# A fused attention and gated MLP kernel on one core: output tiles of 16 by 8 tokens stored by one transfer each, more places for the first chunk's output, and the last accumulator finished by halves

## The chip, the core and the metric

The kernel runs on one core of one Trainium2 chip. The metric is the device time of one execution in microseconds (us). Five engines run side by side, each with its own instruction queue that is worked off in order: TensorE (PE, matmuls; its weight loads are listed as PEld), VectorE (DVE), ScalarE (ACT), GpSimd (POOL) and SyncE (SP). SP computes nothing: it issues nearly all DMA transfers of this kernel. A few transfers are issued from ACT's queue.

## What is computed

Two steps in float32. First an attention over 8 batches, 8 heads, 576 positions and 64 columns per head, that adds a coarse part and a local part. Then its output, seen as 4608 tokens of 512 values, goes through a gated MLP with 2048 hidden units.

```python
# attention, per head: q, k, v are (576, 64)
q_d, k_d, v_d = (t.reshape(144, 4, 64).mean(1) for t in (q, k, v))
out_up    = repeat(softmax(q_d @ k_d.T / 8) @ v_d, 4)          # coarse part
out_local = softmax(where(|i - j| < 4, q @ k.T / 8, -1e9)) @ v  # band of 7
x = (out_up + out_local)          # -> (8 * 576 tokens, 8 * 64 = 512)
# MLP
h = x @ w_in                      # (4608, 2048)
g = h * clip(h + 3, 0, 6) / 6
out = g @ w_out                   # (4608, 512)
```

## The kernel before

**Chunks.** The MLP works on nine chunks of 512 tokens. Chunks 0 to 6 go through `plan_moe` one after the other; the tokens that are left, two chunks' worth, go together through `plan_strassen`, a block multiplication with seven products, which ends the program. The attention of a batch (576 tokens) must be done before the chunk that needs it, and its matmuls come in short bursts between the MLP's matmuls.

**Tokens and batches.** The attention writes a batch transposed: `xt[b]` has the columns of a pair of heads on the partitions and the 576 tokens along the row, in 16 runs (`NC`) of 36 tokens (`RP`). Two places hold batches (`xb`, the first 9216 bytes of each partition and the 9216 behind it): batch 0's leftovers and then the even batches lie in the first one, named `first` in the trace, and the odd batches in the second, named `arena` there as nearly everything else is. Chunk n takes tokens 512 n to 512 n + 511 in order, so that its tokens come from one or two batches.

**Splitting a chunk.** All big matmuls are made of three with rounded operands: x is split into a rounded part and the rest (`plan_split`; the matmuls stay exact enough by hi·hi + hi·lo + lo·hi). For each half of the 512 columns (`k` in steps of two blocks of 128) and each batch in the chunk there is one copy (hi, on ACT or DVE, line 120 or 122) and one subtraction (lo, line 976, on DVE or POOL) into the tile `rounded`. The split waits for the last first-layer matmul of the chunk before, half by half.

**A chunk.** For 16 blocks `f` of 128 hidden units: 12 matmuls into one of two accumulators `h0`, `h1` (line 1060), ACT and DVE make g from it and split it (lines 1066 to 1078), and two blocks later 12 matmuls add its share to the four output accumulators `o0` to `o3` (line 1119), one for each tile of 128 tokens. The attention bursts use `h0` and `h1` too, and free them with the additions of line 757 on DVE.

**Storing.** `plan_store` copies an output accumulator to a place `ob` (lines 1022 on ACT, 1024 on DVE), of which there are two, and SP stores it from there. In DRAM the tokens lie as 36 by 32 rows: token r of run c is row 32 r + c. So a tile of 128 consecutive tokens is stored in pieces that end where a run of 36 ends, four or five transfers a tile (line 1036). A place is free, and the next accumulator can be copied, when its transfers have landed; an accumulator is free for the next chunk when it has been copied.

**The order.** `Plan.emit` plays the program through with costs and due times and writes every engine's queue in the order that it finds. DVE, ACT, POOL and SP work strictly in that order. Operations whose cost table names two engines (`on(...)`) go to the one that is free first. So an edit moves instructions in places that it does not touch. Other work in these queues: `plan_sum` adds weight blocks for the later block multiplication (lines 1177 and 1182) in a place of its own, `so`, and stores them (line 1189, to `si` and `so` in DRAM); the next sum can start when that store has landed. q and k are loaded at line 323 and turned on DVE at line 329.

**The end.** In the block multiplication the second layer ends in accumulators of 128 output columns by 512 tokens. The last product (`plan_units(4, ..., 2)`) adds eight blocks of three matmuls (line 1624) to two accumulators, named `o` in the trace; then `finish` turns each on DVE in two halves of 256 tokens (line 1576), and `plan_out` stores it in four transfers of 32 columns by 512 tokens (line 1589), two from SP and two from ACT, each of which waits for both halves.

Of the kernel before, what the change touches and what calls it, by code (L numbers as in the profile page):

```python
# [8 lines left out]
F32 = mybir.dt.float32  # L9
# [47 lines left out]
def tile_local_down_attention_moe(ctx, tc, q_all, k_all, v_all, _qk_loc, _v_loc, w_in, w_out, ident_d, _mask_d, out):  # L57
# [882 lines left out]
    def x_of(n, b, k, ks, s0, cnt):  # L940
        if n == PAIR0 - 1 and b == B - 2:
            return runs(b, k, ks)[:, :, :EDGE, :LONG]
        if b:
            return xt[b][:, k:k + ks, s0:s0 + cnt]
        return x0[k][:, s0:s0 + cnt].unsqueeze(1) if n == 0 else xt[0, "tail"][:, k:k + ks]

# [4 lines left out]
    def pieces(n):  # L951

        first, size = PART[n]
        if n == 0:
            return [(0, 0, 0, HALF), (0, HALF, HALF, TOK - HALF)]
        out_, t = [], first
        while t < first + size:
            b, s0 = divmod(t, S)
            k = min(S - s0, first + size - t)
            out_.append((b, s0, t - first, k))  # L960
            t += k
        return out_

    def plan_split(n, prev_last):

        ks = 1 if n == 0 else 2

        def part(i, b, k, off, cnt):
            x = parts_of(n)[i][:, k:k + ks, off:off + cnt]
            return x.rearrange("p k (c r) -> p k c r", r=LONG) if n == PAIR0 - 1 and b == B - 2 else x  # L970

        def hi(eng, b, s0, off, cnt, k):
            copy_on(eng, part(0, b, k, off, cnt), x_of(n, b, k, ks, s0, cnt))

        def lo(eng, b, s0, off, cnt, k):
            eng.tensor_tensor(
                part(1, b, k, off, cnt), x_of(n, b, k, ks, s0, cnt), part(0, b, k, off, cnt).bitcast(F32),
                op=ALU.subtract)

        done = []  # L980
        for k in range(0, NK, ks):
            for b, s0, off, cnt in pieces(n):
                free = [("x0", (0, k))] if n == 0 else []
                a = op(on("xhi", ks * cnt), 0, lambda eng, a=(b, s0, off, cnt, k): hi(eng, *a),
                       [x for h in range(k, k + ks) for x in x_done[b, h][s0 // HALF if n == 0 else 0:][:1 if n == 0 else None]]
# [5 lines left out]
                if n and s0 + cnt == S:  # L991
                    last_split.setdefault(b, []).append(c)
        split_done[n] = done
        for b, s0, _, cnt in pieces(n):
            if n and s0 + cnt == S:
                plan.free_after(xb_of(b), last_split[b])
# [1207 lines left out]
```

## Time and profile before

| | |
|---|---|
| median of three runs | 895.48 us |
| the three runs | 895.33, 895.48, 899.03 us |
| the profiled execution | 898.18 us |
| its span, first to last instruction | 896.3 us |
| mean granted TensorE clock in it | 0.996 |
| PE busy | 876.3 us (98%) |
| DVE, ACT, POOL busy | 658.4, 491.2, 291.5 us |
| DMA queue of SP | 354680 packets, 134.48 MB |

The span is what the profiler's views cover; the 1.9 us up to the execution's own time lie around it. A row of a view by lines gives the line in the source, the engine, the operation, the tile written and the tiles read, how many there were, their busy time and the mean of one. A row of the timeline gives the start and the length in us; the bracket at its end is idle time of that engine just before, and what ended it. "SPq" and "ACTq" are transfers being issued by those queues, not the transfers themselves. In a table by stretches each engine has its busy microseconds with the number of instructions behind it, then the granted clock, the share of the 16 DMA engines and what they moved.

### The profile page before, as it was taken

To read this page: it belongs to the slowest core of one execution; us is meant where nothing else is said; L and a number is where in the kernel's file an instruction comes from. 1 tells how busy PE (TensorE), PEld (TensorE's weight loads), DVE (VectorE), ACT (ScalarE), POOL (GpSimd) and SP (SyncE) were. 2 spreads that over 40 slices of the span, in tenths; PEclk is the share of its full clock that TensorE was granted. 3 is DMA by queue.
4 is the path that set the end of the run, shared out by engine and by line. 5 is a ranking of instruction groups with operands and counts; after the bars stand their busy time and mean duration, and the time that the engine had idled before them with its cause. 6 is when DMAs were issued, how large, how long until landed. Compare 5 with 4: busy or idle time off the path is not lost.

```text
span 896.3 us, 19849 instructions
## 1 busy us (share of the span) xinstructions
PE 876.3 (98%) x6913; PEld 714.8 (80%) x6913; DVE 658.4 (73%) x1224; ACT 491.2 (55%) x1542; POOL 291.5 (33%) x383
## 2 busy tenths in 40 slices
PE   6999999999999999999999999999999999999997
PEld 5667778788888888878888888888888888888786
DVE  7898876566666777667857776676757777778983
ACT  4799866455664545535455555454443426556760
POOL 3645542135443342234403351333312111013321
PEclk9899999999999999999999999999999999999999
DMA  9999753456566664656565654777855117564784
GB/s 221 289 221 250 178 141 66 99 116 119 114 142 131 139 143 114 134 124 136 120 139 122 147 124 100 135 213 217 209 130 136 36 37 232 206 218 145 267 266 62
DMA packets 361052, 137.59 MB, mean 154 GB/s; under 512 B 270456, under 2 KB 333048, under 8 KB 360952
## 3 DMA queue, kind: packets, MB, share of 16 engines
q1 hardware_dynamic: 354680, 134.48, 61.1%
q10 hardware_dynamic: 6272, 1.84, 0.9%
q8 instruction: 55, 0.90, 0.4%
q14 instruction: 45, 0.37, 0.1%
HBM read 91.62 MB, written 44.63 MB: 152 GB/s over the span
## 4 chain that ended last, share of the span: by engine, by line
PE 88%; DVE 5%; DMA 2%; SPq 1%; ACT 1%; issue 1%; ACTq 0%; DVEq 0%
PE o L1119 32%; PE h L1060 31%; PE h L1374 4%; PE a L1374 4%; PE o L1624 4%; PE o L1475 2%; PE a L709 2%; PE h L752 1%; PE a L1624 1%; PE h L1624 1%; PE a L501 1%; PE h L664 1%; DMA arena<-in_k_dram 1%; SPq L323 1%; DMA out_dram<-arena 1%
## 5 line engine op out<-in xcount | busy, mean ns | idle before, releaser
L1119 PE MATMUL o<-wp,rounded 128*128 128x512 f32 x1344 | 324.1, 393 | 2.6 <-DVE arena L1024 1.5
L1060 PE MATMUL h<-rounded,wp 128*128 128x512 f32 x1344 | 316.8, 390 | 2.4 <-DVE first L757 1.7
L1060 PEld LDWEIGHTS h<-rounded,wp 128*128 128x128 f32 x1344 | 251.2, 188 | 56.5 <-issue 3.2
L1119 PEld LDWEIGHTS o<-wp,rounded 128*128 128x128 f32 x1344 | 249.5, 188 | 56.7 <-DVE arena L1024 1.9
L1074 ACT CAST rounded<-arena 128x512 fp32r<-128x512 f32 x112 | 69.1, 617 | 73.1 <-PE o L1119 39.9
L1066 ACT ACTIVATE arena<-h 128x512 f32<-128x512 f32 x112 | 66.5, 594 | 75.2 <-PE h L1060 72.4
L1070 DVE SCALAR_TENSOR_TENSOR arena<-arena,h 128x512 f32<-128x512 f32 x112 | 75.8, 678 | 43.2 <-ACT arena L1066 42.5
L1078 DVE TENSOR_TENSOR rounded<-arena,rounded 128x512 fp32r<-128x512 f32 x83 | 60.9, 735 | 42.5 <-PE o L1119 33.2
L565 ACT ACTIVATE arena<-arena 128x64 f32<-128x64 f32 x240 | 80.3, 337 | 0.4
L1078 POOL TENSOR_TENSOR rounded<-arena,rounded 128x512 fp32r<-128x512 f32 x29 | 38.8, 1338 | 70.3 <-PE o L1119 45.2
L329 DVE STREAM_TRANSPOSE arena<-arena 128x576 f32<-128x576 f32 x56 | 43.3, 773 | 20.2 <-DMA arena<-in_q_dram 9.7
L1182 POOL TENSOR_TENSOR arena<-arena 128x128 f32<-128x128 f32 x57 | 31.5, 553 | 76.6 <-DVE arena L1182 33.7
L378 POOL TENSOR_TENSOR arena<-arena 128x144 f32<-128x144 f32 x30 | 13.5, 451 | 111.7 <-DVE arena L329 78.7
L422 POOL TENSOR_TENSOR arena<-arena 32x256 f32<-32x256 f32 (+1 forms) x27 | 22.9, 847 | 72.1 <-DMA arena<-in_v_dram 52.0
L541 ACT ACTIVATE arena<-arena 128x1 f32<-128x1 f32 (+1 forms) x78 | 15.1, 193 | 56.2 <-DVE arena L554 56.2
L565 ACT ACTIVATION_READ_ACCUMULATOR arena<-arena 128x1 f32 x240 | 45.2, 188 | 0.0
L684 ACT ACTIVATE arena<-h 128x144 f32<-128x144 f32 x24 | 7.0, 290 | 66.0 <-PE h L664 66.0
L582 DVE TENSOR_TENSOR arena<-arena 128x640 f32<-128x640 f32 (+1 forms) x43 | 37.5, 875 | 1.1
L380 POOL TENSOR_TENSOR arena<-arena 128x144 f32<-128x144 f32 x60 | 35.4, 590 | 4.7
L1374 PE MATMUL a<-wp,wp 128*128 128x512 f32 x144 | 36.5, 390 | 0.4 <-DVE arena L1404 0.4
L420 DVE TENSOR_REDUCE arena<-arena 128x128 f32<-128x512 f32 (+1 forms) x25 | 26.6, 1066 | 8.0 <-PE h L664 4.1
L1374 PEld LDWEIGHTS a<-wp,wp 128*128 128x128 f32 x144 | 27.0, 188 | 6.3 <-DVE arena L1404 0.8
(281 smaller groups left out, 1385.4 us busy)
## 6 DMA issues: line engine op xcount, KB each, us to landing
rawp<-in_w_in_dram SPq DMA_DIRECT2D x16, 512.0 KB
rawp<-in_w_out_dram SPq DMA_DIRECT2D x16, 512.0 KB
arena<-in_q_dram SPq DMA_DIRECT2D x112, 72.0 KB
arena<-in_k_dram SPq DMA_DIRECT2D x112, 72.0 KB
pl<-arena SPq DMA_DIRECT2D x24, 320.0 KB
arena<-pl SPq DMA_DIRECT2D x96, 80.0 KB
arena<-in_v_dram SPq DMA_DIRECT2D x28, 256.0 KB
wd<-wp SPq DMA_DIRECT2D x12, 512.0 KB
```

The source lines that it names most:

```text
L329: nc.vector.transpose(out=qk[kind], in_=qk[kind])
L380: eng.tensor_tensor(t, t, x[:, :, r], op=ALU.add)
L565: nc.scalar.activation(x[:, j], x[:, j], AF.Exp, bias=m[:, j:j + 1], scale=0.125, accum_out=s[:, j:j + 1])
L582: eng.tensor_tensor(x, x, s.unsqueeze(2).broadcast_to(list(x.shape)), op=ALU.mult)
L1060: nc.tensor.matmul(st["ps"], win[f][:, wt, kk * P:(kk + 1) * P], xs[part][:, kk], start=(kk == 0 and i == 0), stop=(kk == NK - 1 and i == ...
L1066: nc.scalar.activation(st["t"], st["ps"], AF.Relu, bias=3.0)
L1070: nc.vector.scalar_tensor_tensor(out=t, in0=t, scalar=6.0, in1=st["ps"], op0=ALU.min, op1=ALU.mult)
L1074: nc.scalar.copy(st["gh"], st["t"])
L1078: eng.tensor_tensor(st["gl"], st["t"], st["gh"].bitcast(F32), op=ALU.subtract)
L1119: nc.tensor.matmul(otile[n, m], gt[:, ms], wout[f][:, wt], start=(f == 0 and i == 0), stop=(f == NF - 1 and i == 2),)
L1374: nc.tensor.matmul(ps, weight(i, j, wt, kk), xpart(MOVING[j], part)[:, kk], start=first and kk == 0 and x == 0, stop=kk == half - 1 and x ...
L1624: nc.tensor.matmul(places[acc, m], w, z[:, part], start=j == 5 and i == 0 and x == 0, stop=i == NG - 1 and x == 2, skip_group_check=True)
```

## The change

**Blocks.** From batch 1 on a batch is cut along its runs instead of along its tokens: four blocks of 16 runs by 8 tokens (128 tokens), and a rest of 16 runs by 4 tokens (64 tokens). `_regions()` deals them out to chunks 1 to 6; the rests of two neighbouring batches lie side by side and fill a tile of 128. Batch 0 keeps its layout (chunk 0, and its last 64 tokens in chunk 1), and so does what chunk 6 takes of batch 6. Every chunk takes as many tokens from each batch as it did. An output tile of one block goes out in one transfer of 16 by 8 rows, and a pair of rests in two.

**Splits.** `split_ops(n)` makes one copy and one subtraction for each single block or rest (both column blocks of a half at once), and one for each column block where two or three blocks of a batch lie side by side. For chunks 1 to 6 these are 8, 6, 10, 8, 10 and 6 pairs of operations, where there were 4 each.

**Places.** The first chunk's output gets a list of places of its own, `ob0`: the two of `ob` and four more in the place of the even batches.

**The end.** The last product finishes its first accumulator, then adds the last five blocks to the second accumulator in two passes, one for each half of 256 tokens. Each half is turned when its pass is done and is stored in four transfers of 32 columns by 256 tokens.

```diff
+    def regions(n):
+        got = []
+        for off, b, j in REGIONS[n]:
+            if j in range(NC) and got and got[-1][0] == b and got[-1][1] in range(NC):
+                got[-1][2] += 1
+            else:
+                got.append([b, j, 1, off])
+        return got
...
+    def split_ops(n):
...
+                x = runs(b, k, ks)[:, :, :, j * BLOCK:(j + nj) * BLOCK]
+                return x if nj == 1 else x[:, 0].rearrange("p c (j r) -> p j c r", r=BLOCK)
...
+        return [cols(b, j, nj, off, k, ks) for kh in range(0, NK, 2) for b, j, nj, off in regions(n)
+                for ks in [1 if nj > 1 else 2] for k in range(kh, kh + 2, ks)]
...
     def plan_store(n, m, ready, frees):
+        okey = "ob" if n else "ob0"
...
-            st_o[n, m] = ob = buf("ob", (n, m), [P, DM])
+            st_o[n, m] = ob = buf(okey, (n, m), [P, DM])
...
-            for p, k, first in stores(at, P):
                 nc.sync.dma_start(
-                    bass.AP(tensor=out.tensor, offset=out.offset + first, ap=[[32 * DM, k], [1, DM]]),
-                    st_o[n, m][p:p + k])
+                    bass.AP(tensor=out.tensor, offset=first + r * 32 * DM, ap=[[DM, NC], [32 * DM, k], [1, DM]]),
+                    st_o[n, m][p:p + NC * k])
...
-            o = [op("DVE", 0.45, partial(turn_half, i), ready, take=tok) for i in range(2)]
-            plan_out(lambda: copies[name, m], M, t, o, tok)
+            for i in range(2):
+                o = op("DVE", 0.45, partial(turn_half, i), [ends[4, m, i]] if (4, m, i) in ends else ready, take=tok)
+                plan_out(lambda: copies[name, m], M, t, [o], tok, i)
...
-                    nc.tensor.matmul(places[acc, m], w, z[:, part], start=j == 5 and i == 0 and x == 0,
+                    nc.tensor.matmul(places[acc, m][:, ts], w, z[:, part, ts], start=j == 5 and i == 0 and x == 0,
...
-            steps = ... one[:3] + two[:3] + both[3:-2] + one[-2:] + two[-2:] ...
+            steps = ... one[:3] + two[:3] + one[3:] + [(i, (1,), x) for x in range(2) for i in range(3, NG)] ...
...
-        "so": slots["ob"][:1],
+        "so": slots["ob"][:1], "ob0": slots["ob"] + [(xb0 + i * 2048, 2048) for i in range(4)],
```

**What moves in the queues.** Line numbers shift: 976 becomes 995, 1024 becomes 1026, 1060 becomes 1074, 1070 becomes 1084, 1078 becomes 1092, 1119 becomes 1133, 1036 becomes 1044 (batch 0) and 1049, 1189 becomes 1203, 1624 becomes 1642. PE's queue is the same up to the second block of chunk 1, and after that nearly so.

DVE while the first chunk's four output accumulators (`o`) are copied out, before the change; the rows between them are the next blocks' gates (1070) and the attention (329, 575, 582):

```order
250 L329 STREAM_TRANSPOSE arena<-arena 128x576
251 L1024 TENSOR_SCALAR arena<-o_859 128x512
252 L1070 SCALAR_TENSOR_TENSOR arena<-arena,h_2075 128x512
253 L575 RECIPROCAL arena<-arena 128x10
254 L582 TENSOR_TENSOR arena<-arena 128x640
255 L1024 TENSOR_SCALAR arena<-o_878 128x512
256 L1024 TENSOR_SCALAR arena<-o_960 128x512
```

The same place after it:

```order
247 L554 TENSOR_REDUCE arena<-a_1983 128x1
248 L1026 TENSOR_SCALAR first<-o_960 128x512
249 L329 STREAM_TRANSPOSE arena<-arena 128x576
250 L575 RECIPROCAL arena<-arena 128x3
251 L582 TENSOR_TENSOR arena<-arena 128x432
252 L1084 SCALAR_TENSOR_TENSOR arena<-arena,h_2050 128x512
```

Of the three copies on DVE one is left, it writes to `first`, and it stands ahead of the attention's and the gates' rows; the other three are on ACT.

SP at the stores of chunk 2, while chunk 3 begins, before the change; `in_v`, `in_q` and `in_k` are loads for the attention, `pd` and `pl` its rows on the way to DRAM. The next loads of q and k stand two rows further on:

```order
231 L1036 DMA out_dram<-arena 20x512
232 L1036 DMA out_dram<-arena 36x512 x6
233 L1036 DMA out_dram<-arena 20x512
234 L397 DMA arena<-in_v_dram 64x4x128
235 L401 DMA arena<-in_v_dram 64x128
236 L1036 DMA out_dram<-arena 16x512
237 L1036 DMA out_dram<-arena 36x512 x3
238 L1036 DMA out_dram<-arena 4x512
239 L1036 DMA out_dram<-arena 32x512
240 L1036 DMA out_dram<-arena 36x512 x2
241 L1036 DMA out_dram<-arena 24x512
242 L608 DMA pd_2_4436<-arena 64x3x144 x2
```

The same place after it:

```order
223 L1049 DMA out_dram<-arena 16x8x512 x2
224 L397 DMA arena<-in_v_dram 64x4x128
225 L401 DMA arena<-in_v_dram 64x128
226 L323 DMA arena<-in_q_dram 32x18x32 x4
227 L1049 DMA out_dram<-arena 16x8x512
228 L608 DMA pd_2_4408<-arena 64x3x144 x2
229 L1049 DMA out_dram<-arena 16x8x512
230 L323 DMA arena<-in_k_dram 32x18x32 x4
```

Seventeen transfers have become four, and the loads of q and k stand between them instead of behind them. In the whole program the stores of chunks 0 to 6 go from 124 transfers to 49.

PE's end before the change; `o_8618` is the first of the last two accumulators and `o_8646` the second:

```order
1877 L1624 MATMUL o_8618<-rounded,wp_1534 128x512 x3
1878 L1624 MATMUL o_8646<-rounded,wp_1534 128x512 x3
1879 L1624 MATMUL o_8618<-rounded,wp_1708 128x512 x3
1880 L1624 MATMUL o_8618<-wp_949,wp_1758 128x512 x3
1881 L1624 MATMUL o_8646<-rounded,wp_1708 128x512 x3
1882 L1624 MATMUL o_8646<-wp_949,wp_1758 128x512 x3
```

And after it, with `o_8584` as the first and `o_8610` as the second:

```order
1875 L1642 MATMUL o_8610<-rounded,wp_1249 128x256 x3
1876 L1642 MATMUL o_8584<-wp_949,wp_1758 128x512 x3
1877 L1642 MATMUL o_8610<-rounded,wp_1437 128x256 x3
1878 L1642 MATMUL o_8610<-rounded,wp_1534 128x256 x3
1879 L1642 MATMUL o_8610<-rounded,wp_1708 128x256 x3
1880 L1642 MATMUL o_8610<-wp_949,wp_1758 128x256 x3
1881 L1642 MATMUL o_8610<-rounded,wp_1249 128x256 x3
1882 L1642 MATMUL o_8610<-rounded,wp_1437 128x256 x3
```

Behind the first accumulator's last matmul stood 6 matmuls of 512 columns; now 27 of 256 columns stand there, the last nine of which follow the rows shown.

More of the change, by code (lines that the diff above doesn't have):

```diff
@@ L964, in plan_split @@
-    def plan_split(n, prev_last):
[L966 to L978, printed above, removed]
-        done = []
[L981 to L985, printed above, removed]
-                       + ((prev_last[:1] if k < NK // 2 else prev_last[1:]) if len(prev_last) == 2 else prev_last),
-                       free=free, dl=start_of(n) - 1.0)
-                c = op(on("xlo", ks * cnt), 0,
-                       lambda eng, a=(b, s0, off, cnt, k): lo(eng, *a), [a], lock=True, free=free)
-                done.append(c)
-                if n and s0 + cnt == S:
-                    last_split.setdefault(b, []).append(c)
@@ L993, in plan_split @@
         split_done[n] = done
-        for b, s0, _, cnt in pieces(n):
-            if n and s0 + cnt == S:
+        for b in last_split:
+            if b < B - 2 and max(m for m in REGIONS if any(b == x[1] for x in REGIONS[m])) == n:
                 plan.free_after(xb_of(b), last_split[b])
@@ L1040, in plan_store @@
[L1040 to L1041 removed]
+            for p, b, j in mine:
+                bp, b2 = divmod(b, NB2)
+                first = out.offset + (bp * NI * P + b2 * NC) * DM
+                if j == "edge":
+                    for c in range(EDGE):
+                        nc.sync.dma_start(
+                            bass.AP(tensor=out.tensor, offset=first + c * DM, ap=[[32 * DM, LONG], [1, DM]]), st_o[n, m][c * LONG:(c + 1) * LONG])
+                    continue
+                if b == 0:
+                    t = n * TOK + m * P
+                    while p < (P // 2 if n else P):
+                        c, r = divmod(t + p, RP)
+                        k = min(RP - r, P - p)
+                        nc.sync.dma_start(
+                            bass.AP(tensor=out.tensor, offset=first + (r * 32 + c) * DM, ap=[[32 * DM, k], [1, DM]]), st_o[n, m][p:p + k])
+                        p += k
+                    continue
+                r, k = (LONG, RP - LONG) if j == "rest" else (j * BLOCK, BLOCK)
+                nc.sync.dma_start(
+                    bass.AP(tensor=out.tensor, offset=first + r * 32 * DM, ap=[[DM, NC], [32 * DM, k], [1, DM]]),
+                    st_o[n, m][p:p + NC * k])
@@ L1043, in plan_moe @@
+        nd = sum(EDGE if j == "edge" or n + b == 0 else 2 if b == 0 else 1 for _, b, j in mine)
+        e = op(on("ob", 1.0), 0, ev, [ready], take=[(okey, (n, m))], free=[frees], dl=start_of(n + 1) + TF * LAG)
+        op("SP", 2.0, store, [e], free=[(okey, (n, m))], size=dma(P, 2048), dl=start_of(n + 1) + 10, nd=nd)
     def plan_moe(n):
```

117 lines of the change are left out of this document (66 added, 51 removed).

## The prediction

> **What bounds the kernel now.** I read the page first, then PE's busy time in stretches of 20 us, then who PE waited for, and then the timeline around each wait.
>
> ```profile
> span 896.3 us, 19849 instructions
> PE 876.3 (98%) x6913; PEld 714.8 (80%) x6913; DVE 658.4 (73%) x1224; ACT 491.2 (55%) x1542; POOL 291.5 (33%) x383
> PE 88%; DVE 5%; DMA 2%; SPq 1%; ACT 1%; issue 1%; ACTq 0%; DVEq 0%
> ```
>
> PE is busy for 98% of the span and carries 88% of the chain of waits. So only idle PE time can be won, 20 us in all, and the stretches say where it lies:
>
> ```profile
> 0.00:20.00 20.00, 13.18 (x172) 10.61 (x172) 13.71 (x34) 8.39 (x27) 7.27 (x18) 1.00 0.89 223
> 20.00:40.00 20.00, 18.76 (x294) 12.28 (x293) 16.71 (x47) 15.72 (x52) 13.90 (x18) 0.83 1.07 253
> 160.00:180.00 20.00, 18.50 (x82) 14.92 (x80) 9.21 (x15) 8.30 (x32) 1.58 (x2) 1.00 0.42 101
> 380.00:400.00 20.00, 18.51 (x180) 15.07 (x179) 13.96 (x29) 6.03 (x22) 7.91 (x13) 1.00 0.53 122
> 820.00:840.00 20.00, 18.97 (x83) 14.98 (x82) 18.29 (x25) 14.35 (x27) 8.61 (x6) 1.00 0.58 192
> 880.00:900.00 20.00, 10.56 (x47) 8.42 (x45) 2.68 (x6) 0.00 (x0) 0.00 (x0) 0.93 0.38 53
> ```
>
> The first number behind the comma is PE's busy time. In the first two rows PE lacks 8 us, at the start, where PE's queue is not changed. Then come three holes, of 1.5, 1.5 and 1.0 us, and the end, where PE stops at 890.56 us and the span goes on to 896.28. The third hole lies in the block multiplication, whose PE order stays nearly as it is: I cost it at nothing either way. The other two and the end are what the change can reach.
>
> **Part 1, places for the first chunk's output.** The hole at 172 us:
>
> ```profile
> 157.44 0.60 ACT L1022 ACTIVATE arena<-o 128x512 f32<-128x512 f32 x1 [0.58 <-PE o L1119]
> 159.30 5.60 PE L1060 MATMUL h<-rounded,wp 128*128 128x512 f32 x24
> 165.39 0.69 DVE L1024 TENSOR_SCALAR arena<-o 128x512 f32<-128x512 f32 x1 [0.20 <-DMA out_dram<-arena]
> 169.38 0.69 DVE L1024 TENSOR_SCALAR arena<-o 128x512 f32<-128x512 f32 x1 [1.72 <-DMA out_dram<-arena]
> 173.13 0.69 DVE L1024 TENSOR_SCALAR arena<-o 128x512 f32<-128x512 f32 x1 [3.06 <-DMA out_dram<-arena]
> 173.88 6.42 PE L1119 MATMUL o<-wp,rounded 128*128 128x512 f32 x27 [1.50 <-DVE arena L1024]
> 183.92 0.81 DVE L757 TENSOR_TENSOR first<-h,arena 128x288 f32<-128x288 f32 x2
> ```
>
> The four copies stand 16 us apart, because each waits for a place whose store has to land; PE needs the fourth accumulator and waits 1.50 us. With six places for four tiles none waits. The copies then need three times 0.60 us on ACT and 0.69 on DVE and are done by about 161 us, while PE has 24 first-layer matmuls to do until 164.9. The whole 1.5 us go, and nothing is late next on PE. The new places lie where batch 2 is written first at 183.9 us. The 20 transfers from them take about 10 us of SP behind 161 (0.5 each, from the SP rows below), and the longest wait above for a landing is 3.06: they have landed by 174 or so, and 10 us are left. **-1.5 us** (bounds 0 and -1.5, the wait itself).
>
> **Part 2, one transfer for each tile.** The hole at 397 us:
>
> ```profile
> 354.08 4.44 SPq L1036 DMA_DIRECT2D out_dram<-arena  x8
> 359.97 3.80 SPq L1036 DMA_DIRECT2D out_dram<-arena  x9
> 380.18 2.40 POOL L1182 TENSOR_TENSOR arena<-arena 128x128 f32<-128x128 f32 x4 [2.37 <-DVE arena L1177]
> 382.07 2.15 SPq L323 DMA_DIRECT2D arena<-in_q_dram  x4
> 388.42 0.59 SPq L1189 DMA_DIRECT2D si<-arena  x1
> 393.47 0.76 DVE L1177 TENSOR_TENSOR arena<-wp 128x256 f32<-128x256 f32 x2 [3.09 <-DMA si<-arena]
> 398.40 0.81 DVE L757 TENSOR_TENSOR first<-h,arena 128x288 f32<-128x288 f32 x2
> 398.99 3.23 PE L1060 MATMUL h<-rounded,wp 128*128 128x512 f32 x13 [1.49 <-DVE first L757]
> ```
>
> PE waits for the additions that free `h0`. DVE came late to them since it stood 3.09 us at a weight sum that waits for the store of the sum before (`si`). POOL had that sum ready at 382.6, but its store went out at 388.4, behind the loads of q and k: In SP's queue ahead of them lie 17 output transfers, 8.24 us. Four transfers at the same 0.48 us take 1.9, so SP is 6.3 us earlier behind them, and the store of the sum, which the new queue has ahead of the k load, goes out soon after 382.6 and has landed before DVE asks. The 3.09 us on DVE go, and with them PE's wait: **-1.5 us**. The other bound is 0: SP's loads may be held by their places and not by the queue. I take the gain, because 8.24 us of issue stand in this very queue, and the chain of waits runs through SP's issues there, one behind the other. Elsewhere the 75 transfers fewer are worth nothing, as PE does not wait for loads there.
>
> **Part 3, the smaller splits.** Each chunk from 1 on has 6 to 10 pairs of operations for 4. What covers them is the rest of the second layer, before PE comes to the new chunk:
>
> ```profile
> L976 DVE TENSOR_TENSOR rounded<-arena,rounded 128x896 fp32r<-128x896 f32 x2 | 2.2, 1092 | 0.4 <-ACT rounded L120 0.4
> L976 DVE TENSOR_TENSOR rounded<-first,rounded 128x128 fp32r<-128x128 f32 x2 | 0.6, 294 | 0.1
> L976 POOL TENSOR_TENSOR rounded<-arena,rounded 128x384 fp32r<-128x384 f32 x1 | 1.0, 1016 | 2.3 <-DVE rounded L122 2.3
> 145.68 1.09 DVE L976 TENSOR_TENSOR rounded<-arena,rounded 128x896 fp32r<-128x896 f32 x1
> 147.24 5.44 PE h L1060 x24
> 243.83 1.05 POOL L976 TENSOR_TENSOR rounded<-arena,rounded 128x256 fp32r<-128x256 f32 x1
> 246.88 5.60 PE L1060 MATMUL h<-rounded,wp 128*128 128x512 f32 x24
> ```
>
> On DVE a subtraction costs 161 ns and 1.04 ns a column (from the first two rows). Chunk 1: the splits end at 146.8 now, their second half is needed at 147.24 + 1.36 = 148.6. DVE's share goes from 3.2 us (2 x 1.09, 2 x 0.29 and two copies) to 3.7 (3 x 0.29, 3 x 0.56 and four copies, some 0.3 each), and one copy of the second half now stands ahead of the first half's subtractions and waits for its matmuls, an estimated 0.6: the splits end near 147.9, still covered, with 0.7 us left. Chunk 2: three of POOL's subtractions are now all of the first half, two of them with 384 columns; the first is the same as now (243.83 to 244.88), the two behind it end at 246.91, where PE begins at 246.88: with a hop between the engines 0.2 us. At chunks 3 to 6 24 more second-layer matmuls (5.4 us) lie between in PE's queue, and two to six operations at 0.16 us more are hidden by them; without that cover they would cost at most 1 us each. **+0.2 us** (bounds 0 and +2).
>
> **Part 4, the end.** From 888 us:
>
> ```profile
> 890.04 2.24 SPq L1589 DMA_DIRECT2D out_dram<-first  x4
> 890.05 2.34 ACTq L1589 DMA_DIRECT2D out_dram<-first  x4
> 890.59 0.78 DVE L1576 STREAM_TRANSPOSE first<-o 128x256 f32<-128x256 f32 x2 [0.58 <-PE o L1624]
> 891.00:892.00 1.00, 0.00 (x0) 0.00 (x0) 0.37 (x2) 0.00 (x0) 0.00 (x0) 1.00 0.98 133
> 894.00:895.00 1.00, 0.00 (x0) 0.00 (x0) 0.00 (x0) 0.00 (x0) 0.00 (x0) 1.00 0.74 104
> L346 PE MATMUL o<-ident,rows 128*128 128x128 f32 x17 | 2.1, 276 | 0.0
> L1624 PEld LDWEIGHTS o<-wp,wp 128*128 128x128 f32 x108 | 20.3, 188 | 4.2
> 868.80 21.77 PE o L1624 x96
> ```
>
> Now all 512 KB of the two accumulators cross after PE's end: 0.8 us of turning, then transfers that keep the DMA engines full (0.98) from 891.0 to 894.75, and 1.5 us to the last instruction: 5.7 us behind PE. After the change the first accumulator is done 27 small matmuls ahead of the end, and half of the second 15 ahead. Only a quarter of the bytes, 0.94 us at the old rate, has to follow PE's end; ahead of it come half the turning (0.43) and two issues a queue (1.1) with 0.9 us from issue to first bytes, where the transfers overlap the issuing. That makes 0.4 + 1.1 + 1.2 + 1.5 = 4.2, a gain of 1.5.
>
> Its price: 15 matmuls of 512 columns (21.77 / 96 = 0.227 us each, 3.4 us) become 30 of 256. No row has one of 256 with such weights. From below, half of 0.227; from above, the 0.188 us of a weight load if each has to wait for it. The nearest row is that of 17 matmuls with 128 columns, each with 128 weight columns loaded: 2.1 / 17 = 0.124. I take 0.124: 30 x 0.124 = 3.7, so +0.3 (bounds 0 and +2.2). Net **-1.2 us**.
>
> The Trainium skill speaks on this point ("TensorE: Matmul & The Clock Gate", section "LDWEIGHTS (loading the stationary operand)"): a load takes its columns over 1.2 GHz, whatever streams afterwards. That would be an estimated 107 ns, just under a matmul of 256 columns, so that halving would cost next to nothing, and the end would gain 1.5 instead of 1.2 us. The trace's 512-column step of 227 ns does not test this.
>
> **The sum.** -1.5 - 1.5 + 0.2 - 1.2 = -4.0 us. The profiled execution's own 898.18 would become 894.2. It lies 2.7 above the median, so I take the sum from the median: 895.48 - 4.0 = **891.5 us**. About 0.5% (4.5 us) is what a measurement of this kernel can tell from no change; the sum lies just inside.
>
> **The rivals.**
> - *The second hole stays, or a new one takes its place.* For it: every queue behind chunk 1 is planned anew, and DVE's waits for sum stores and loads can fall ahead of any other burst; the list of waits has seven of them for `si`:
>
> ```profile
> DVE arena L1177 <- DMA si<-arena: 9.8, 7, 3.1
> ```
>
>   Against it: SP's relief holds in all chunks. It gives 895.48 - 2.5 = 893.0, with a second such hole 894.5.
> - *The small matmuls run at the pace of weight loads.* 30 x 0.188 = 5.6 instead of 3.4 makes the end lose 0.7: -2.1 in all, 893.4. The PEld row speaks for it, L346's 0.124 against it.
> - *Slower: reading blocks of 8 tokens makes the splits slow.* DVE's 3.7 us of chunk 1's splits, twice as slow, would end at 151.6, and PE wait 3.0 us; POOL's chain at chunk 2 would end 3.1 later: -4.0 + 6.1 = +2.1, 897.6. It decides from a factor of about 1.7 on. Nothing in the rows shows such a factor, but none has pieces of 8.
> - *The gain is there and cannot be seen.* The clock row of 20 to 40 us (0.83) means 3.4 us of clock withheld at the start, and the runs lie 3.7 us apart. If the median falls among the longer runs: 898.18 - 4.0 = 894.2.
>
> **How the numbers follow.** My forecast 0.45, its own range 889.5 to 893; the hole that stays or moves 0.25; the weight loads 0.12; the longer runs 0.12; the slow splits 0.06. The range 889 to 896 leaves out the last and the tips. Faster by over 0.5% means under 891.0: a little under half of the forecast's case, and a part of the second where the third hole goes too, 0.25. Slower, over 900.0: the slow splits at a larger factor or several new holes, 0.05. Within: 0.70.
>
> **What would show it.** The copies 1026 without waits for `out_dram`, and no wait of PE for them. No PE hole near 395 us, and the sum stores issued within 1 us of POOL's last addition. PE's first-layer steps of chunks 1 and 2 without a wait for lines 120, 122 or 995. Thirty matmuls of 256 columns in 3.7 us, and 4.2 us from PE's end to the span's. I am wrong if a hole of over 1 us stands at a new place, or the small matmuls take over 0.16 us.

## The result, and the profile after

The kernel after takes 891.06 us (median of 6 runs, 890.71 to 893.43), the kernel before 896.80 on the same chip (6 runs, 895.33 to 899.03). The ratio is 0.994 with a 95% interval of 0.9921 to 0.9959. The forecast was 891.5. The gain of 0.6% lies at the bound of what can be told from no change (0.5%), and the interval reaches to both sides of it.

The profiled execution after took 890.71 us with a span of 888.9, against 898.18 and 896.3 before. First its page:

```profile
span 888.9 us, 19832 instructions
PE 873.9 (98%) x6928; PEld 715.5 (80%) x6928; DVE 658.2 (74%) x1221; ACT 491.3 (55%) x1554; POOL 306.2 (34%) x414
PE 93%; DVE 3%; ACT 2%; DMA 1%; issue 0%; ACTq 0%; SPq 0%; DVEq 0%
```

Then the table by stretches of the kernel after (columns as before):

```profile
20.00:40.00 20.00, 18.88 (x351) 12.84 (x351) 19.60 (x53) 17.69 (x59) 15.27 (x19) 1.00 1.02 256
160.00:180.00 20.00, 20.00 (x187) 16.60 (x186) 8.84 (x15) 8.55 (x32) 4.56 (x7) 1.00 0.35 94
380.00:400.00 20.00, 20.00 (x187) 16.61 (x186) 14.27 (x31) 9.72 (x40) 7.34 (x14) 1.00 0.54 117
820.00:840.00 20.00, 18.98 (x83) 15.00 (x82) 19.04 (x30) 14.58 (x26) 3.83 (x3) 1.00 0.74 253
```

PE is now 93% of the chain of waits, and SP's issues are gone from it. The holes at 172 and 397 us are closed; the one in the block multiplication stands as it was (18.98 of 20 us busy).

**Where the time went, by marks.** A wait's bracket tells how long PE stood, not how much later everything became. For that I used marks: the start of the same group of 40 small attention matmuls (line 752) in burst after burst, which the traces show at 27 places. The kernels are compared from the first mark behind 70 us on, which lies at 82.47 us before and at 80.00 after.

| piece of the span | before | after | difference |
|---|---|---|---|
| up to the first mark | 82.47 | 80.00 | -2.47 |
| first mark to the mark behind chunk 0 (180.65, 176.40) | 98.18 | 96.40 | -1.78 |
| to 344.39, 339.81 | 163.74 | 163.41 | -0.33 |
| to 415.94, 409.59 | 71.55 | 69.78 | -1.77 |
| to 705.13, 698.35 | 289.19 | 288.76 | -0.43 |
| to the last product's accumulators `o` (868.63, 861.85) | 163.50 | 163.50 | 0 |
| those to PE's end (890.56, 884.77) | 21.93 | 22.92 | +0.99 |
| PE's end to the span's end | 5.74 | 4.13 | -1.61 |
| sum | 896.3 | 888.9 | -7.40 |

The first row isn't the change's: the profiled execution before had part of its clock withheld there (0.83 between 20 and 40 us, 1.00 after), and one and the same later kernel ("crossed", below) had its first mark at 78.52 in one execution and at 82.00 in another. Without it the change took 4.93 us from this pair of executions, against 5.7 at the medians and a forecast of 4.0.

**Chunk 0's output.** Timeline of the kernel after (the time since the first mark is shorter by what the table says, so look at the order of the rows and not at the clock alone):

```profile
155.00 1.97 ACT L1024 ACTIVATE first<-o 128x512 f32<-128x512 f32 x3 [0.58 <-PE o L1133]
156.85 5.60 PE L1074 MATMUL h<-rounded,wp 128*128 128x512 f32 x24
157.21 0.68 DVE L1026 TENSOR_SCALAR first<-o 128x512 f32<-128x512 f32 x1
```

The four copies that stood 16 us apart are now done within 3 us and wait for no landing. PE's 24 first-layer matmuls run through.

**The sum's store.** SP, POOL and DVE of the kernel after around the place of the second hole:

```profile
349.64 1.25 SPq L1049 DMA_DIRECT2D out_dram<-arena  x2
355.67 0.58 SPq L1049 DMA_DIRECT2D out_dram<-arena  x1
357.71 0.56 SPq L1049 DMA_DIRECT2D out_dram<-arena  x1
...
373.82 2.40 POOL L1196 TENSOR_TENSOR arena<-arena 128x128 f32<-128x128 f32 x4 [1.18 <-DVE arena L1191]
377.82 0.54 SPq L1203 DMA_DIRECT2D si<-arena  x1
381.60 0.72 DVE L1191 TENSOR_TENSOR arena<-wp 128x256 f32<-128x256 f32 x2
391.42 0.81 DVE L757 TENSOR_TENSOR first<-h,arena 128x288 f32<-128x288 f32 x2
```

Four output transfers stand where 17 stood. The sum's store goes out at 377.82, where it was 388.42: 10.6 us earlier, of which 4.6 are the lead of the whole program there, so 6.0. DVE's sum at 381.60 has no bracket; it waited 3.09 us before.

**The end.** The timeline of the kernel after:

```profile
880.58 1.23 PE L1642 MATMUL o<-rounded,wp 128*128 128x256 f32 x9
880.77 0.78 DVE L1590 STREAM_TRANSPOSE arena<-o 128x256 f32<-128x256 f32 x2 [6.41 <-PE o L1642]
881.25 4.84 SPq L1605 DMA_DIRECT2D out_dram<-arena  x8
882.56 0.45 DVE L1590 STREAM_TRANSPOSE arena<-o 128x256 f32<-128x256 f32 x1 [1.01 <-PE o L1642]
883.07 1.14 PEld L1642 LDWEIGHTS o<-rounded,wp 128*128 128x128 f32 x9 [0.74 <-DVE arena L1590]
883.07 1.34 PE L1642 MATMUL o<-rounded,wp 128*128 128x256 f32 x9 [0.54 <-DVE arena L1590]
884.25 0.52 PE L1642 MATMUL o<-wp,wp 128*128 128x256 f32 x3
884.80 0.45 DVE L1590 STREAM_TRANSPOSE arena<-o 128x256 f32<-128x256 f32 x1 [1.79 <-PE o L1642]
```

And two stretches of 1 us behind PE's end (the number before the last is the share of the DMA engines):

```profile
885.00:886.00 1.00, 0.00 (x0) 0.00 (x0) 0.25 (x1) 0.00 (x0) 0.00 (x0) 1.00 0.15 22
886.00:887.00 1.00, 0.00 (x0) 0.00 (x0) 0.00 (x0) 0.00 (x0) 0.00 (x0) 1.00 0.75 104
```

The tail shrinks by 1.61 us. Its price shows in two brackets: PE stands for 0.54 us (its weight loads for 0.74) in front of the last half, until DVE has turned the first half of the same accumulator (882.56 + 0.45). In the tail the DMA engines are now nearly idle for 1 us (0.15): in that microsecond the end waits for turning and issuing, not for bytes.

### The profile page after: what moved, and what is told of

Read it like the earlier page. It is cut to its first block, busy times and chain, and to the rows that moved or that the text cites. A ratio compares the mean times of both kernels' runs of the same rounds, so it can differ in the third digit from the quotient of the medians.

```text
span 888.9 us, 19832 instructions
## 1 busy us (share of the span) xinstructions
PE 873.9 (98%) x6928; PEld 715.5 (80%) x6928; DVE 658.2 (74%) x1221; ACT 491.3 (55%) x1554; POOL 306.2 (34%) x414
## 4 chain that ended last, share of the span: by engine, by line
PE 93%; DVE 3%; ACT 2%; DMA 1%; issue 0%; ACTq 0%; SPq 0%; DVEq 0%
PE o L1133 35%; PE h L1074 33%; PE h L1388 4%; PE o L1642 4%; PE a L1388 4%; PE a L1642 2%; PE o L1489 2%; PE a L709 2%; PE h L752 2%; PE a L501 1%; PE h L664 1%; DMA arena<-in_k_dram 1%; PE o L346 0%; PE h L501 0%; ACT early L547 0%
## 5 line engine op out<-in xcount | busy, mean ns | idle before, releaser
L1092 DVE TENSOR_TENSOR rounded<-arena,rounded 128x512 fp32r<-128x512 f32 x75 | 57.6, 769 | 46.0 <-PE o L1133 38.1
L1092 POOL TENSOR_TENSOR rounded<-arena,rounded 128x512 fp32r<-128x512 f32 x37 | 49.6, 1340 | 96.5 <-PE o L1133 53.5
L1196 POOL TENSOR_TENSOR arena<-arena 128x128 f32<-128x128 f32 x68 | 34.3, 504 | 69.6 <-DVE arena L1196 31.0
L1388 PE MATMUL h<-wp,wp 128*128 128x512 f32 x144 | 35.5, 390 | 0.3 <-DVE arena L1418 0.3
L582 DVE TENSOR_TENSOR arena<-arena 128x640 f32<-128x640 f32 (+1 forms) x42 | 33.4, 798 | 1.2
L380 POOL TENSOR_TENSOR arena<-arena 128x144 f32<-128x144 f32 x52 | 30.9, 594 | 4.1
L1388 PEld LDWEIGHTS h<-wp,wp 128*128 128x128 f32 x144 | 27.0, 188 | 6.3 <-DVE arena L1418 0.8
L1457 POOL TENSOR_TENSOR arena<-arena 128x512 f32<-128x512 f32 x9 | 17.1, 1900 | 42.1 <-DVE arena L1426 16.3
```

Source lines behind the costliest of these rows:

```text
L582: eng.tensor_tensor(x, x, s.unsqueeze(2).broadcast_to(list(x.shape)), op=ALU.mult)
L1092: eng.tensor_tensor(st["gl"], st["t"], st["gh"].bitcast(F32), op=ALU.subtract)
L1196: eng.tensor_tensor(u[:, z], u[:, x], u[:, y], op=o)
L1388: nc.tensor.matmul(ps, weight(i, j, wt, kk), xpart(MOVING[j], part)[:, kk], start=first and kk == 0 and x == 0, stop=kk == half - 1 and x ...
```

## The experiments

The theory was the forecast's: three separate gains, at 172 us by the places, at 397 by SP's time, and at the end by the halves. The main rival was that every edit makes the planner write all queues anew, so that holes open and close wherever they like. The table gives how much later than in the kernel after each profiled execution was, in us, at marks and at PE's end, all counted from the first mark; below it the tail and the median of the runs.

| mark (us in the kernel after) | before | no places | whole end | four stores | runs layout | two stores | one, told four | crossed | places only | after again | crossed again |
|---|---|---|---|---|---|---|---|---|---|---|---|
| 176 | 1.78 | 1.07 | 0.02 | -0.02 | -0.02 | 0.02 | -0.01 | -0.01 | -0.02 | 0.02 | 0.03 |
| 252 | 1.78 | 1.83 | 0.76 | 0.71 | -0.02 | 0.01 | 0.76 | -0.01 | -0.03 | 0.74 | 0.05 |
| 313 | 1.78 | 1.83 | 0.76 | 3.80 | 0.00 | 0.71 | 0.76 | -0.01 | 2.44 | 1.18 | 0.15 |
| 388 | 2.10 | 1.82 | 0.76 | 5.93 | 0.69 | 1.95 | 0.76 | -0.01 | 2.93 | 1.24 | 0.21 |
| 410 | 3.88 | 1.83 | 0.77 | 8.09 | 0.70 | 1.96 | 0.76 | 0.00 | 3.00 | 1.25 | 0.22 |
| 678 | 4.30 | 1.91 | 1.03 | 19.72 | 4.34 | 4.06 | 0.69 | 0.15 | 3.92 | 1.32 | 0.22 |
| PE's end | 3.32 | 2.03 | 0.03 | 19.72 | 5.00 | 4.23 | 0.72 | -0.41 | 3.67 | 1.33 | -0.37 |
| tail (after: 4.13) | 5.74 | 3.99 | 5.89 | 3.83 | 3.78 | 3.92 | 4.00 | 4.12 | 5.70 | 4.11 | 4.20 |
| median (after: 891.06) | 896.80 | 893.37 | 892.59 | 908.43 | 893.32 | 896.47 | 891.28 | 890.51 | 894.23 | 891.14 | 891.97 |

The medians carry the start's scatter of 3 to 4 us, and the kernels ran in four groups, in which the kernel before had medians of 896.80, 895.99, 895.01 and 896.09; the marks have neither. But they hold what clock was withheld behind the first mark: some 3.4 us of the last two rows of "four stores" (0.83 between 660 and 680 us) and 1.9 of those of "runs layout". Tails are good to 0.05 us, since the span is given to 0.1.

**No places.**

```diff
-        okey = "ob" if n else "ob0"
+        okey = "ob"
```

> The kernel after, with the first chunk's output in the two places that all other chunks use. Theory (the six places close the hole at 172 us): the four copies of the accumulators wait for landings of their stores again, 0.2 to 3 us each, PE waits about 1.5 us for the fourth, and the time is 1.5 to 1.8 us above the kernel after (about 892.4 where that has 890.7). Rival (the new order of the work closed the hole, whatever the places): no PE wait near 168 us, within 0.3 us of the kernel after.

The timeline of this kernel at chunk 0's output:

```profile
163.63 0.69 DVE L1026 TENSOR_SCALAR arena<-o 128x512 f32<-128x512 f32 x1
167.63 0.69 DVE L1026 TENSOR_SCALAR arena<-o 128x512 f32<-128x512 f32 x1 [0.83 <-DMA out_dram<-arena]
171.37 0.69 DVE L1026 TENSOR_SCALAR arena<-o 128x512 f32<-128x512 f32 x1 [3.04 <-DMA out_dram<-arena]
172.11 3.24 PE L1133 MATMUL o<-wp,rounded 128*128 128x512 f32 x13 [0.80 <-DVE arena L1026]
```

The copies spread out again over 16 us and wait for landings, and PE waits 0.80 us for the last one: 1.07 us at the mark, less than the 1.5 to 1.8 expected, since the last copy came 0.7 us earlier than before. The ratio to the kernel before is 0.9967 (0.9954 to 0.9980). The theory holds, its size was too large. The 0.76 at the next mark is another matter, told under "whole end".

**Places only** (the kernel before with the new places and nothing else; diff as in the part of the change on `plan_store` and the list of places).

> The kernel before with the places for the first chunk's output and nothing else. Theory: the hole at 172 us goes whole, 1.78 us on the attention's marks behind it (1.50 of waiting and 0.28 of starting again), the holes near 320, 397 and 613 and the tail of 5.7 stay: 1.5 to 1.8 us below the kernel before. Rival (the wait turns up elsewhere, at chunk 1 or in the loads): less than 0.8 us at the mark near 270 us.

The hole is gone whole: 1.80 us at the first mark behind it, as far as the mark at 275. Then the rival has its say. In the list of PE's waits stands

```profile
PE h L1060 <- DVE arena L757: 2.5, 3, 1.8
```

which the kernel before does not have; the longest of them is at 300.92 us. By the mark at 313 the gain is given back and 0.66 more, the hole at 397 closes by the new plan, and at the mark at 678 0.38 us are left in this execution. At PE's end it is 0.35 later than the kernel before: there PE waits 0.47 us in the last product (at 879.76 us, for DVE at line 1560), which the kernel before does not do. The runs say 0.9981 (0.9966 to 0.9997). So the places take away the hole that they should, and the planner then moves the other holes.

**Whole end.**

```diff
-            steps = ... one[:3] + two[:3] + one[3:] + [(i, (1,), x) for x in range(2) for i in range(3, NG)] ...
+            steps = ... one[:3] + two[:3] + both[3:-2] + one[-2:] + two[-2:] ...
-            for i in range(2):
-                o = op("DVE", 0.45, partial(turn_half, i), [ends[4, m, i]] if (4, m, i) in ends else ready, take=tok)
-                plan_out(lambda: copies[name, m], M, t, [o], tok, i)
+            o = [op("DVE", 0.45, partial(turn_half, i), ready, take=tok) for i in range(2)]
+            plan_out(lambda: copies[name, m], M, t, o, tok)
```

> The kernel after, with the last accumulator in whole matmuls and whole stores as in the kernel before. Theory (the halves take 1.6 us from the tail and give 0.2 back in small matmuls and 0.5 in PE's wait for the turning of the first half): PE's end to the span's end goes from 4.1 back to 5.7 us, PE's wait of 0.5 goes, the time is 0.8 to 1.1 us above the kernel after. Rival (the tail is set by something after the stores, not by their bytes): tail 4.1 as well, and 0.7 us below the kernel after.

The tail is 5.89 again (+1.76), and from the mark at 678 to PE's end 1.00 us are saved (1.03 to 0.03): the halves are worth 0.76 us net. The median is 1.5 above the kernel after, and some 0.75 of that is no part of the end: every engine's queue is the same as in the kernel after until the end begins, and yet this execution is 0.76 us late at chunk 2. The timeline at the splits there, first in this kernel:

```profile
239.86 2.30 POOL L995 TENSOR_TENSOR rounded<-first,rounded 128x384 fp32r<-128x384 f32 x2
241.21 1.23 DVE L995 TENSOR_TENSOR rounded<-arena,rounded 128x256 fp32r<-128x256 f32 x1
242.13 1.47 POOL L1092 TENSOR_TENSOR rounded<-arena,rounded 128x512 fp32r<-128x512 f32 x1
242.37 1.64 DVE L995 TENSOR_TENSOR rounded<-first,rounded 128x384 fp32r<-128x384 f32 x1
244.06 4.35 PE L1074 MATMUL h<-rounded,wp 128*128 128x512 f32 x17 [0.25 <-DVE rounded L995]
```

And in the kernel after:

```profile
241.51 0.53 DVE L995 TENSOR_TENSOR rounded<-first,rounded 128x384 fp32r<-128x384 f32 x1
241.66 2.07 POOL L995 TENSOR_TENSOR rounded<-first,rounded 128x384 fp32r<-128x384 f32 x1 [0.21 <-DVE rounded L122]
241.97 0.40 DVE L995 TENSOR_TENSOR rounded<-arena,rounded 128x256 fp32r<-128x256 f32 x1
242.31 0.54 DVE L995 TENSOR_TENSOR rounded<-first,rounded 128x384 fp32r<-128x384 f32 x1
```

The same subtraction of 384 columns takes 0.54 us on DVE or 1.64, and about 1.0 on POOL or 2.07. When DVE's three come first, POOL's is the long one and nobody waits for it; when POOL is in between, DVE's are, and PE waits. In the first fence DVE's 1.64 ends at 244.01, which is 0.41 behind the end of POOL's 1.47 (243.60): it seems to have stood while POOL worked and to have run afterwards.

**After again** (the same kernel once more).

> The kernel after once more, on the chip of the two below. Three kernels with its order of the first chunks were 0.75 us late at chunk 2's splits, two were not. Theory (it is a matter of which of DVE and POOL takes a subtraction first, not of the order): this profile may show either, marks up to 230 us and from 275 us on as before, or all 0.75 later; median 890.5 to 892.

The median is 891.14, the ratio 0.9951 (0.9935 to 0.9967). Its profile shows the other case: 0.74 us late at chunk 2, with DVE's subtractions at 1.28, 1.23 and 1.64 us, and 0.5 more between the marks at 291 and 340. So one program has both timings. Of the nine profiles with these splits and places in chunk 2, five are late by 0.7 to 0.8 us ("no places" among them), and four are not.

**Subtractions on DVE** (chunk 2's subtractions not offered to POOL).

```diff
-            c = op(on("xlo", cnt), 0, ...
+            c = op({e: v for e, v in on("xlo", cnt).items() if n != 2 or e == "DVE"}, 0, ...
```

> The kernel after with all six subtractions of chunk 2's splits on DVE, none on POOL. Three kernels with the splits of the kernel after show PE late by 0.75 us there, with subtractions of 384 columns at 1.64 us on DVE while POOL subtracts too, and 0.54 while it does not. Theory (the two engines slow each other): each takes 0.40 to 0.55 us on DVE, PE does not wait for line 995, and the shift at chunk 2 is 0 to 0.3. Rival (DVE is slow there for its own reasons, or is now too full): subtractions over 0.8 us, or PE waits 0.3 us or more there.

The timeline of this kernel at chunk 2's splits:

```profile
243.58 1.30 POOL L1092 TENSOR_TENSOR rounded<-arena,rounded 128x512 fp32r<-128x512 f32 x1 [1.76 <-ACT rounded L1088]
243.87 1.42 DVE L995 TENSOR_TENSOR rounded<-first,rounded 128x384 fp32r<-128x384 f32 x1
245.55 1.01 DVE L995 TENSOR_TENSOR rounded<-first,rounded 128x384 fp32r<-128x384 f32 x2
```

Five of the six take 0.41 to 0.55 us; the one that meets POOL's subtraction of line 1092 takes 1.42. That is the mutual hindrance once more, with another partner, so "each 0.40 to 0.55" was wrong in one of six. PE does not wait for line 995, but the new plan opens a hole of 0.8 us elsewhere (for line 757, at 260 to 280 us): PE's end is 1.76 us later than in the kernel after, the median 893.98, the ratio 0.9987 (0.9972 to 1.0001). Nothing is won.

**Four stores.**

```diff
-                nc.sync.dma_start(
-                    bass.AP(tensor=out.tensor, offset=first + r * 32 * DM, ap=[[DM, NC], [32 * DM, k], [1, DM]]),
-                    st_o[n, m][p:p + NC * k])
+                for c in range(0, NC, NC // 4):
+                    nc.sync.dma_start(
+                        bass.AP(tensor=out.tensor, offset=first + (r * 32 + c) * DM, ap=[[DM, NC // 4], [32 * DM, k], [1, DM]]),
+                        st_o[n, m][p + c * k:p + (c + NC // 4) * k])
-        nd = sum(EDGE if j == "edge" or n + b == 0 else 2 if b == 0 else 1 for _, b, j in mine)
+        nd = sum(EDGE if j == "edge" or n + b == 0 else 2 if b == 0 else 4 for _, b, j in mine)
```

> The kernel after with each 16 by 8 block (and each rest) stored by four transfers of 4 by 8 tokens for one, and the planner told so: same bytes, same layout, same splits, some 150 transfers more on SP. Theory (SP's issue time opened the hole at 397 us): the sum store near 378 us goes out some 3 to 5 us later, DVE waits for it again, PE waits 1 to 1.5 us near 390: 1.0 to 1.5 us above the kernel after. Rival (the new order of SP's queue, with the sum store ahead of the k loads, closed it, and issue time has slack): within 0.3 us of the kernel after.

**One, told four** (only the last line of that diff, the planner's number; the orders of DVE, ACT, POOL and PE are those of "four stores", row for row, and SP's but for the transfers).

> The kernel with four transfers for each block, order for order, but with one transfer in the place of the four: the planner is told four, as there, so that every engine's row of work is the same. Theory (SP's issue time made the 17 us): all PE waits at lines 757 and 1133 between 270 and 660 us go, within 1 us of the kernel after. Rival (the other order made for four transfers is what is slow): PE waits stay, 5 us or more above the kernel after.

**Two stores** (`NC // 2` for `NC // 4`, and 2 for the 4).

> The kernel after with two transfers for each block or rest (74 output transfers of chunks 0 to 6 for 49, where four for each gave 124 and 17 us more). Theory (each transfer costs SP 0.4 to 0.65 us, and PE waits only where a queue of loads is late; slack is used up first): 0 to 3 us above the kernel after, far less than a third of the 17 us. Rival (the cost is in the transfers' form, pieces of 4 by 8 tokens being slow to land, not in SP's time): a third of it, 5 to 6 us.

Four stores: 908.43, ratio 1.0141 (1.0118 to 1.0165). One, told four: 891.28, ratio 0.9965 (0.9952 to 0.9979). The same order with one transfer in the place of four is 17.2 us faster at the medians (of two groups; 16 by the ratios), and no wait of PE for line 757 or at line 1133 is left in it between 270 and 660 us: here it is the transfers and not the plan, and far more than I had expected. Two stores: 896.47, ratio 1.0018 (1.0001 to 1.0036), 5.4 above the kernel after (4.2 by the marks) and not the 0 to 3 of the theory; the number is the rival's, 5 to 6.

At the place of the second hole these two kernels can be compared row by row. One, told four:

```profile
383.99 0.54 SPq L1203 DMA_DIRECT2D si<-arena  x1
389.80 0.75 DVE L1191 TENSOR_TENSOR arena<-wp 128x256 f32<-128x256 f32 x2
```

Four stores:

```profile
389.75 0.54 SPq L1204 DMA_DIRECT2D si<-arena  x1
394.83 0.76 DVE L1192 TENSOR_TENSOR arena<-wp 128x256 f32<-128x256 f32 x2 [3.32 <-DMA si<-arena]
```

Counted from the mark at 388 the sum's store goes out 4.0 us later with four transfers (the 3 to 5 of the theory), DVE waits for it again, and PE waits 1.88 us behind that, where it waited 1.49 before the change. From chunk 2's output transfers (353 us) to that store SP has no pause of over 0.11 us between two issues with four transfers, and none in the kernel before either; with one transfer it pauses four times, for 3.0 us together. So at this place it is SP's issue time. What the transfers cost elsewhere is seen in what the traces say of the line that stores (ns for one issue: lowest, median, highest; then first and last start). Before, with runs:

```profile
L1036 SPq DMA_DIRECT2D out_dram<-arena x120: 257/364/2042, 162.3 to 743.0; - x120
```

After, with blocks:

```profile
L1049 SPq DMA_DIRECT2D out_dram<-arena x25: 539/566/596, 253.2 to 734.0; - x25
```

Four stores:

```profile
L1050 SPq DMA_DIRECT2D out_dram<-arena x100: 615/616/786, 253.7 to 757.5; - x100
```

Two stores:

```profile
L1050 SPq DMA_DIRECT2D out_dram<-arena x50: 603/632/1272, 253.2 to 738.9; - x50
```

At the medians a run of up to 36 tokens costs SP 364 ns, a block of 16 by 8 tokens 566, and a quarter of it still 616. So the quarters add 100 x 0.616 - 25 x 0.566 = 47.4 us to SP's queue, the halves 50 x 0.632 - 14.2 = 17.4: at the medians each of these microseconds cost 0.36 and 0.31. In four stores DVE waits 13.5 us for the sums' stores to `si`, where the kernel after has 3.3 and "one, told four" 5.9, and PE waits for the additions behind it; from the list of PE's waits of four stores:

```profile
PE h L1075 <- DVE first L757: 6.0, 4, 1.9
PE h L1075 <- DVE arena L757: 4.5, 3, 2.1
PE o L1134 <- ACT arena L1024: 2.9, 1, 2.9
```

The third row is a copy that waits for a landing (3.56 us, at 666 us), so landings have a share in the 17 us.

**Runs layout** (the kernel before with the places and with the end by halves, without blocks).

> The kernel before with the places for the first chunk's output and the end by halves, so without the blocks: old splits, 124 output transfers. Theory (blocks are worth 1.5 us by the hole at 397, and their smaller splits cost nothing): the hole at about 392 us is there, 1.5 us above the kernel after, PE waits 1.5 for the additions of chunk 3. Rival (any new plan closes that hole): within 0.3 us of the kernel after. If the smaller splits cost something, it is below the kernel after.

893.32, ratio 0.9970 (0.9953 to 0.9986), 2.3 above the kernel after. But the hole is not where the theory put it: nothing opens at 388 to 410, 0.7 us at 313 to 340, and the large one is at 609.63 us, by the timeline of this kernel:

```profile
609.63 7.31 PE L1060 MATMUL h<-rounded,wp 128*128 128x512 f32 x24 [1.83 <-DVE first L757]
```

The chain of waits ahead of it runs through 4 us of q and k loads on SP (line 323), a sum's store and the 4 us until a load of v has landed. Of the 3.7 us that this execution loses there, 1.9 are clock (the 24 matmuls take 7.31 us for 5.44, at a granted 0.91). In each of the three kernels without blocks (before, places only, this one) the chain of waits ahead of the large hole runs through SP's issues and through landings, and the plan says where the hole stands.

**Crossed.** The wait in front of the last half is there because DVE reads the accumulator that PE writes next. Crossing the halves of both accumulators puts other work there:

```diff
-            steps = ... one[3:] + [(i, (1,), x) for x in range(2) for i in range(3, NG)] ...
+            steps = ... [(i, (m,), x) for x in range(2) for m in range(2) for i in range(3, NG)] ...
```

> The kernel after with both of the last accumulators by halves and crossed: first half of the one, first half of the other, second half of the one, second half of the other (60 matmuls of 256 columns for 30, and 15 of 512 fewer). Theory (PE waits 0.74 us in front of the last half because that half writes the accumulator that DVE is still turning; a half of the other accumulator, 1.8 us, covers it): the wait for line 1590 goes, the small matmuls cost 0.25 us more, the tail stays near 4.1: 0.3 to 0.6 us below the kernel after. Rival (the tail is set by the 16 transfers' issue, 4.8 us a queue): the later stores crowd behind PE's end, tail 4.5 or more, no gain.

The end of this kernel in the timeline:

```profile
881.28 1.24 PE L1642 MATMUL o<-rounded,wp 128*128 128x256 f32 x9
881.48 0.45 DVE L1590 STREAM_TRANSPOSE arena<-o 128x256 f32<-128x256 f32 x1 [1.35 <-PE o L1642]
882.36 0.52 PE L1642 MATMUL o<-wp,wp 128*128 128x256 f32 x3
```

No PE row has a bracket any more. Up to 603 us this execution agrees with the kernel after to 0.11 us at every mark; PE's end is 0.41 us earlier and the tail the same. The 60 small matmuls run from 875.53 to 882.88 and start 0.120 us apart (nine of them from 881.28 to 882.36). The theory holds. The median is 890.51, the ratio 0.9952 (0.9939 to 0.9964).

**Crossed again**, beside the kernel after.

> The kernel with crossed halves once more, beside the kernel after on one chip. Theory: 0.4 us less from the last accumulators' start to the span's end (0.74 of waiting saved, 0.25 to 0.35 of small matmuls spent), at medians 0 to 1 us below the kernel after, which 5 rounds may not tell apart. Rival: no difference or slower.

PE's end is again 0.37 us earlier (0.6 from the mark at 678 on), the tail 4.20. At the medians it stands at 891.97, the kernel after at 891.14, with first marks at 82.00 and 79.99 in the two profiles. The traces show 0.4 us in favour of crossing at PE's end and 0.6 behind the mark at 678, twice; the medians can't show it.

## Why the prediction was right, and where its steps were not

The time came within 0.5 us of the forecast, and the pieces sum to 4.93 us for a forecast 4.0, but not by the terms that I had written down. That the time came so near is luck in part: at the medians the change took 5.7 us, but the kernel before, too, had a median 1.3 us above the one that I started from.

- **Part 1, -1.5.** Right in mechanism and place, and shown by two edits: places alone take 1.80 us there, their absence costs 1.07. The size was off by 0.28: a wait of 1.50 us made everything 1.78 later. At each of the two large holes the mark lost 0.28 more than the bracket shows, and all terms taken from a bracket of PE lack this. The starts of single matmuls at 173.88 us tell where it goes: 0.16 of it, because a matmul's row lasts 0.389 us where the next one otherwise starts 0.227 behind it, so that the bracket begins too late; 0.11, because the second matmul behind the hole starts 0.339 behind the first.
- **Part 2, -1.5.** The hole closed: four transfers for 17, the sum's store 6.0 us earlier (forecast 6.3), no wait of DVE, 1.77 us. The store went out 1.6 us behind POOL's last addition (376.22 to 377.82), not within 1 us, since loads of q stand ahead of it. That SP's issue time can make this hole is shown by four stores against one, told four. That it alone made it before is not shown: in "runs layout" and "places only" all 17 transfers stayed, the store went out only 0.6 and 1.3 us earlier by the marks than before, and the hole at 397 closed all the same. In "runs layout" DVE had the store's landing 3.4 us after its issue (383.27 to 386.67), in the kernel before 5.05 after (388.42 to 393.47); what made the landing shorter stays open.
- **Part 2, elsewhere.** "Elsewhere the 75 transfers fewer are worth nothing" was the step that failed: the kernels with runs all have a hole of over 1 us, but at 397 us (before), 300 (places only) or 610 (runs layout), so the rival of a hole that moves came true wherever the plan changed and the runs stayed. Of the six kernels with blocks in one transfer each, none has a wait of PE of over 1 us between 180 and 700 us, and one (subtractions on DVE) has one of 0.8. So that the hole *stays closed* was luck in part. Two small losses, near 320 and 613 us, went as well, 0.33 and 0.43 in the table; that they are the change's is not shown, as the same kernel lost 0.50 and 0.18 there in its second profile.
- **Part 3, +0.2.** It was 0 in the profile after and 0.75 in the same kernel again. The step that failed was to give each subtraction one duration. The row of before with 1.09 us for 896 columns was one in which no instruction of POOL was under way when DVE began. The splits of chunk 1 ended at 145.96 with their second half needed at 144.61 + 1.36 = 145.97: covered, with nothing of the 0.7 us left that I had counted.
- **Part 4, -1.2.** The tail gained 1.61 (forecast 1.5), and the small matmuls start 0.12 us apart (forecast 0.124; nine of them from 880.58 to 881.65, and 0.120 in "crossed"). What failed is a term that is missing: PE's wait for the turning of the first half, 0.54 us at the bracket and 0.79 in the sum (the 0.99 of the table less 0.20 for the small matmuls). With it the end is worth 0.62, and "whole end" gave 0.76.
- The Trainium skill's rule on weight loads ("TensorE: Matmul & The Clock Gate", section "LDWEIGHTS (loading the stationary operand)") gave an estimated 107 ns for the weight load of a small matmul, and with it a halving that costs next to nothing. The measured step of 120 ns lies above it, and halving cost 30 x 0.120 - 15 x 0.227 = 0.20 us, where the row of 128 columns had given 0.3.
- **The other rivals.** Strided splits are not slow: 384 columns in 0.54 us is 161 ns and 1.0 ns a column, the price of before. The weight-load pace of 0.188 did not come.

What stays open: why runs, which need some 22 us more of SP than blocks (120 x 0.364 against 25 x 0.566 + 20 x 0.364, the 20 being batch 0's), cost only 2 to 3 us, where 17 us more for two stores cost 4 to 5. Queue positions differ in every plan, and but for the one place in four stores, landings were not separated from issues.

## What to carry to other kernels

Count a queue's load in issue time by the form of the transfer and not in transfers or bytes, and look at what stands behind the long stretches of it. In a program whose orders are planned anew at each edit, compare by marks, the same instruction group in both traces, rather than by waits: a hole that is gone may stand elsewhere. When a result is finished by parts, ask of each part who still reads the buffer that the next part writes, and put other work between.

## What the runs showed of the hardware

- DVE and POOL hold each other up while both subtract from memory to memory: 0.54 us became 1.64 on DVE, 1.01 became 2.07 on POOL, and which of them pays changed from run to run of one program. The Trainium skill says so ("SBUF — State Buffer", section "Who interferes with whom"): a VectorE instruction with two inputs in SBUF contends with a GpSimd instruction that reads SBUF, for a pair of ports that only one of the two can hold. The traces agree: DVE's 1.64 us (whole end) and its 1.42 (subtractions on DVE) both ended 0.41 us behind POOL's instruction.
- Issue time does not go by bytes: an output transfer of 16 by 8 rows (256 KB) held SP's queue for 566 ns at the median, one of 4 by 8 rows (a quarter of that) for 616, one of up to 36 rows for 364. What in the form decides was not separated: a load of v with 64 rows in two dimensions (line 401) took 612 ns in the kernel after.
- The clock is withheld once in some executions, and not always at the start: 0.83 in the stretch of 20 to 40 us (before), 0.91 at 600 to 620 (runs layout), 0.83 at 660 to 680 (four stores), and in others, the kernel after among them, nowhere before PE's end. The two late ones begin within 1.2 us of the end of a wait of PE, of 1.83 and of 2.87 us; other waits, of up to 2.05 us in four stores, had none near them.
